# Chunked attention and a Fourier-mixing MLP: the MLP's scheduling priority, the queue of the output DMAs, and the order around the column transform

## The chip, the cores and the metric

The kernel runs on one core of a Trainium2 chip. The metric is the device time of one execution in microseconds (us). The core has TensorE (PE, matmuls and transposes), VectorE (DVE), ScalarE (ACT), GpSimd (POOL) and SyncE (SP, here only a queue that issues DMAs). Each engine works through its own instructions in a fixed order and waits at one whose inputs are not there yet; the engines wait for each other by semaphores. SBUF is the working memory of all engines, PSUM the memory into which TensorE writes; PSUM's buffers are few, and their reuse makes waits.

## The reference

Four batches of 768 rows and 8 heads of 64 (so 512 columns). First an attention in chunks of 32 rows, each chunk looking at 16 rows before it, 8 rows after it and 8 memory rows; then a Fourier mixing, a normalization and an MLP:

```python
for c in range(nc):
    q_c = q[:, :, c_start:c_end]
    k_full = np.concatenate([mem_k, k[:, :, l_start:r_end]], axis=2)
    v_full = np.concatenate([mem_v, v[:, :, l_start:r_end]], axis=2)
    a = softmax(scale * q_c @ k_full.T)
    out[:, :, c_start:c_end] = a @ v_full
x = out.transpose(0, 2, 1, 3).reshape(B, S, H * D)
u = x + np.real(np.fft.fft(np.fft.fft(x, axis=1), axis=2))
un = (u - mean(u)) / np.sqrt(var(u) + 1e-06)
return u + np.maximum(un @ w_ch1, 0.0) @ w_ch2
```

Only float32 goes in and comes out: 4x768x512 is written.

## The kernel before, in words

For each batch there are three stages.

**Attention** (`emit_keys`, `emit_pair`) goes by pairs of heads, four pairs a batch, n = 0 to 15 over all. `emit_keys(n)` loads q, k and v (DMAs on SP's queue), casts q and k to bf16 (L239 into `qb`, L241 into `kb`), copies a shifted part of v (L245, POOL), transposes q on TensorE (L250 into the PSUM tile `trq`), copies it out on ACT (`qT`, L252), transposes k (L256 into `trk`) and copies that out on ACT (`kTb`, L261). `trq` and `trk` have the same tag "tr" with one buffer, so `trk` waits for the copy of `trq`. `emit_pair(n)` then does two halves g: scores (L279, `sc`, one buffer), the exponential (L284, ACT), the product with v (L293, `xa`, one buffer; a float32 matmul is two records in the trace), the reciprocal and the scaled copy on DVE (L297 `zs`, L298 `xsb`), which frees `xa`. In batch 0 the cast of q is DVE's and that of k POOL's; later both are POOL's.

**Fourier mixing** (`emit_fx`): a fold of the batch on DVE for each of two parities (`zy` L313, `pq`, `ff` L321 and L322), split into two float16 parts (`hi` on ACT L326, `lo` on DVE L327), the row transform (`ps`, L335 and L342), its two float16 parts (`up` L349 and L350, `dn` L352), and then for each of six row tiles kt the column transform (`pm`, 8 matmuls, L364), the addition to x on DVE (L368), mean and variance (L370, L371), the subtraction (`un` L373), four transposes (`tp`, L376) and their copy (`unT`, L377). `ps`, `pm` and `tp` share the tag "acc" with two PSUM buffers.

**MLP** (`emit_mlp`): two halves of 384 rows; for each 16 groups of four matmuls (`ph`, L391) with a ReLU on ACT (`hT`, L394), then three groups of 16 matmuls (`pc`, L399), the result on DVE (`osb`, L402) and the output DMA on SP's queue (L404). `ph` and `pc` share the tag "mlp" with two PSUM buffers.

The source emits, for b = 0 to 3, attention(b+1), mixing(b+1) and then MLP(b). A scheduler orders the instructions of each engine: among those that it takes to be ready it picks the one with the highest priority, by default the one that was emitted earlier. So MLP(b), which needs only its own batch, is what fills TensorE while batch b+1 is in attention and mixing. MLP(3) has nothing after it. The weights are loaded by eight DMAs on POOL's queue during attention of batch 0.

Of the kernel before, what the change touches and what calls it, by code (L numbers as in the profile page):

```python
# [10 lines left out]
FP32 = mybir.dt.float32  # L11
BF16 = mybir.dt.bfloat16
FP16 = mybir.dt.float16
# [22 lines left out]
def kernel(  # L36
# [11 lines left out]
    nc = tc.nc  # L48
# [183 lines left out]
    def emit_keys(n):  # L232

        b, pr = seq[n]
        emit_loads(n)
        qb = apool.tile([QP, RB, 2, D], BF16, tag="qb", bufs=1, name="qb")
        kb = apool.tile([KP, RB, 2, D], BF16, tag="kb", bufs=1, name="kb")
        eng = nc.vector if b == 0 else nc.gpsimd
        eng.tensor_copy(qb.rearrange("p j h d -> p h j d"),  # L239
                        qf[n % NS].rearrange("p h (j d) -> p h j d", j=RB))  # L240
        nc.gpsimd.tensor_copy(kb.rearrange("p j h d -> p h j d"),  # L241
                              kf[n % NS].rearrange("p h (j d) -> p h j d", j=RB))
        for hh in range(2):
            v1 = va[(2 * n + hh) % NV]
            nc.gpsimd.tensor_copy(v1[96:128, 0:NT, 0:D + 1], v1[0:32, 1:NB, 0:D + 1])  # L245
        kT = kTb[n % NKT]
        qT = apool.tile([P, S], BF16, tag="qT", bufs=2, name="qT")
        trq = aps.tile([P, S], BF16, tag="tr", bufs=1, name="trq")
        for j in range(RB):
            nc.tensor.transpose(trq[:, j * QP:(j + 1) * QP],  # L250
                                qb[:, j].rearrange("p h d -> p (h d)"), ident_b[0:QP, 0:QP])
        nc.scalar.copy(qT.rearrange("p (a j) -> p a j", j=RB),  # L252
                       trq.rearrange("p (j a) -> p a j", j=RB))
        trk = aps.tile([P, RB * KP], BF16, tag="tr", bufs=1, name="trk")
        for j in range(RB):
            nc.tensor.transpose(trk[:, j * KP:(j + 1) * KP],  # L256
                                kb[:, j].rearrange("p h d -> p (h d)"), ident_b[0:KP, 0:KP])
        nc.vector.tensor_copy(
            kT.rearrange("p (b c) -> p b c", b=NB)[:, 0:NT, 64:72],
            mkT[:, b * (H // 2) + pr, :].unsqueeze(1).to_broadcast([P, NT, NMEM]))  # L260
        nc.scalar.copy(  # L261
            strided(kT, 0, [[BS, NB], [8, 8], [1, RB]]),
            strided(trk, 0, [[8, NB], [1, 8], [KP, RB]]))
        qT_of[n], kT_of[n] = qT, kT

    def emit_pair(n):
        b, pr = seq[n]
        h = 2 * pr
        if b not in xs:
            xs[b] = apool.tile([P, NST, DM], FP32, tag="xsb", bufs=3, name=f"xsb{b}")  # L270
        xb = xs[b]
        qT, kT = qT_of.pop(n), kT_of.pop(n)
        for g in range(2):
            sc = aps.tile([P, 2, 8, 64], FP32, tag="sc", bufs=1, name="sc")
            for t6 in range(6):
                t = 6 * g + t6
                for hh in range(2):
                    r0 = 64 * hh
                    nc.tensor.matmul(sc[:, hh, t6, :], kT[r0:r0 + 64, t * BS:t * BS + P],  # L279
                                     qT[r0:r0 + 64, ts(t, 64)], start=True, stop=True,  # L280
                                     tile_position=(r0, 0))
            e1 = apool.tile([P, 2, 6, 64], FP32, tag="e1", bufs=3, name="e1")
            for half in range(2):
                nc.scalar.activation(e1[:, :, :, ts(half, 32)], sc[:, :, 0:6, ts(half, 32)],  # L284
                                     AFT.Exp, bias=mbias[:, half:half + 1],
                                     scale=1.0 / math.sqrt(D))
            xa = aps.tile([P, 3, 2, 66], FP32, tag="xa", bufs=1, name="xa")
            for st in range(3):
                for hh in range(2):
                    v1 = va[(2 * n + hh) % NV]  # L290
                    for half in range(2):
                        t6 = 2 * st + half
                        nc.tensor.matmul(xa[64 * half:64 * half + 64, st, hh, 0:65],  # L293
                                         e1[:, hh, t6, :], v1[:, 6 * g + t6, 0:65],
                                         start=True, stop=True)
            zs = apool.tile([P, 3, 2], FP32, tag="zs", bufs=3, name="zs")
            nc.vector.reciprocal(zs, xa[:, :, :, 64])  # L297
            nc.vector.tensor_tensor(  # L298
                xb[:, 3 * g:3 * g + 3, h * D:(h + 2) * D].rearrange("p s (h d) -> p s h d", h=2),
                xa[:, :, :, 0:D], zs.unsqueeze(3).to_broadcast([P, 3, 2, D]), ALU.mult)  # L300
# [3 lines left out]
    def emit_fx(b):  # L304
# [48 lines left out]
                rr.append((up.rearrange("p i k s -> p i (k s)"), dn))  # L353
        mu_s = fpool.tile([P, NST, 2], FP32, tag="mu", bufs=2)
        unT = fpool.tile([P, NDT, S], FP16, tag="unT", bufs=2, name="unT")
        for kt in range(NST):
            pm = fps.tile([P, 2, HD], FP32, tag="acc", name="pm")
            for par in range(2):
                im = 0
                for ab in range(2):  # L360
                    rhs = cosD if ab == 0 else (nsinD if kt < 3 else sinD)
                    for part in range(2):
                        lhs = rr[2 * par + ab][kt // 3][:, part, ts(kt % 3, P)]
                        nc.tensor.matmul(pm[:, par, :], lhs, rhs[:, par, :],  # L364
                                         start=(im == 0), stop=(im == 3))
                        im += 1
            uv = xb[:, kt, :].rearrange("p (j c) -> p c j", c=2)
            nc.vector.tensor_tensor(uv, pm, uv, ALU.add)  # L368
            st6 = fpool.tile([P, 6], FP32, tag="st6", bufs=3)
            nc.vector.bn_stats(st6, xb[:, kt, :])  # L370
            nc.vector.bn_aggr(mu_s[:, kt, :], st6)  # L371
            un = fpool.tile([P, DM], FP16, tag="un", bufs=3)
            nc.vector.tensor_scalar(un, xb[:, kt, :], mu_s[:, kt, 0:1], None, ALU.subtract)  # L373
            tp = fps.tile([P, NDT, P], FP16, tag="acc", name="tp")
            for dt in range(NDT):
                nc.tensor.transpose(tp[:, dt, :], un[:, ts(dt, P)], ident_h)  # L376
            nc.vector.tensor_copy(unT[:, :, ts(kt, P)], tp)  # L377
        rstd = fpool.tile([P, NST], FP32, tag="rstd", bufs=2)
        nc.gpsimd.tensor_scalar(rstd, mu_s[:, :, 1], eps, None, ALU.add)  # L379
        nc.gpsimd.tensor_tensor(rstd, rstd, mhalf, ALU.pow)  # L380
# [2 lines left out]
    def emit_mlp(b):  # L383
        xb = xs[b]
        unT, rstd = us[b]
        for sh in range(2):
# [8 lines left out]
            for stl in range(3):  # L395
                st = sh * 3 + stl
                pc = fps.tile([P, DM], FP32, tag="mlp", name="pc")
                for ht in range(NHT):
# [2 lines left out]
                osb = fpool.tile([P, DM], FP32, tag="osb", bufs=3)  # L401
                nc.vector.scalar_tensor_tensor(osb, pc, rstd[:, st:st + 1], xb[:, st, :],  # L402
                                               ALU.mult, ALU.add)
                nc.sync.dma_start(out[b, ts(st, P), :], osb)  # L404

    HP = H // 2

# [13 lines left out]
    for b in range(B):  # L421
        if b + 1 < B:
            emit_attention(b + 1)
            emit_fx(b + 1)
        emit_mlp(b)


# [28 lines left out]
```

## Time and profile before

| | us |
|---|---|
| median of 3 runs (lowest, highest) | 374.26 (372.51, 374.93) |
| the profiled execution | 372.16 |
| its span, from the first to the last instruction | 370.4 |
| TensorE busy | 302.9 (82%) |
| VectorE busy | 196.7 (53%) |
| ScalarE busy | 148.6 (40%) |
| GpSimd busy | 82.6 (22%) |

The profile is of one execution. Its page gives busy time by engine, the span in 40 slices, and the chain of work that ended last: 60% of it is TensorE's, 24% VectorE's. The trace behind it holds each instruction with its start and length and what ended the idle time before it. A matmul's record runs on after the next one has begun, so a stream of matmuls is priced by the length of the whole stream over its count.

### The profile page before, as it was taken

To read this page: it belongs to the slowest core of one execution; us is meant where nothing else is said; L and a number is where in the kernel's file an instruction comes from. 1 tells how busy PE (TensorE), PEld (TensorE's weight loads), DVE (VectorE), ACT (ScalarE), POOL (GpSimd) and SP (SyncE) were. 2 spreads that over 40 slices of the span, in tenths; PEclk is the share of its full clock that TensorE was granted. 3 is DMA by queue.
4 is the path that set the end of the run, shared out by engine and by line. 5 is a ranking of instruction groups with operands and counts; after the bars stand their busy time and mean duration, and the time that the engine had idled before them with its cause. 6 is when DMAs were issued, how large, how long until landed. Compare 5 with 4: busy or idle time off the path is not lost.

```text
span 370.4 us, 6887 instructions
## 1 busy us (share of the span) xinstructions
PE 302.9 (82%) x2848; PEld 188.6 (51%) x2848; DVE 196.7 (53%) x372; ACT 148.6 (40%) x258; POOL 82.6 (22%) x97
## 2 busy tenths in 40 slices
PE   0126661775999999999999999799999994799995
PEld 0125551664755465566554665575545552454542
DVE  8952328966632179787221598763213976541001
ACT  1554441452375166225733642347235430151430
POOL 7712660630064030112730101127000000010000
PEclk9999999987899999999999999999999997699999
DMA  7995699955110230159802004491010000000102
GB/s 132 195 164 114 127 225 196 232 98 127 31 27 2 94 94 2 37 165 180 139 28 80 23 0 126 119 181 22 31 40 18 28 30 28 2 0 28 58 6 79
DMA packets 42022, 30.65 MB, mean 83 GB/s; under 512 B 30216, under 2 KB 32264, under 8 KB 41992
## 3 DMA queue, kind: packets, MB, share of 16 engines
q1 hardware_dynamic: 39304, 26.03, 33.9%
q0 software_dynamic: 2688, 4.19, 6.2%
q8 instruction: 22, 0.36, 0.5%
q14 instruction: 8, 0.07, 0.1%
HBM read 28.11 MB, written 6.29 MB: 93 GB/s over the span
## 4 chain that ended last, share of the span: by engine, by line
PE 60%; DVE 24%; ACT 7%; issue 5%; POOL 2%; SPq 1%; DMA 0%; POOLq 0%; ACTq 0%; DVEq 0%
PE pc L399 17%; PE ph L391 16%; PE xa L293 10%; PE pm L364 6%; DVE zy L313 4%; ACT e L284 3%; PE ps L335 3%; PE sc L279 2%; PE tp L376 2%; DVE pq L315 2%; DVE st L370 2%; DVE lo L327 2%; PE trq L250 2%; DVE xsb L368 2%; DVE pq L316 2%
## 5 line engine op out<-in xcount | busy, mean ns | idle before, releaser
L391 PE MATMUL ph<-unT,w_sb 128*128 128x384 f16 x512 | 95.4, 328 | 1.7 <-DVE osb L402 0.8
L394 ACT ACTIVATE hT<-ph 128x384 f16<-128x384 f32 x128 | 62.1, 492 | 79.8 <-PE ph L391 79.7
L399 PE MATMUL pc<-w_sb,hT 128*128 128x512 f16 x384 | 90.0, 380 | 0.0
L391 PEld LDWEIGHTS <-w_sb 128*128 128x128 f16 x512 | 47.8, 98 | 37.8 <-issue 9.8
L399 PEld LDWEIGHTS <-hT 128*128 128x128 f16 x384 | 35.9, 98 | 38.7 <-issue 0.7
L293 PE MATMUL xa<-va,e 128*64 128x65 f32 x768 | 42.1, 257 | 8.9 <-issue 5.9
L402 DVE SCALAR_TENSOR_TENSOR osb<-pc,rstd,xsb 128x512 f32<-128x512 f32 x24 | 18.0, 748 | 53.2 <-PE pc L399 53.2
L293 PEld LDWEIGHTS xa<-va,e 128*64 128x64 f32 x768 | 33.9, 164 | 21.1 <-issue 16.0
L284 ACT ACTIVATE e<-sc,mbias 128x384 f32<-128x384 f32 x64 | 33.7, 578 | 23.0 <-PE sc L279 22.8
L297 DVE RECIPROCAL zs<-xa 128x6 f32<-128x6 f32 x32 | 6.1, 192 | 61.7 <-PE xa L293 61.6
L245 POOL COPY va<-va 32x780 f32<-32x780 f32 x32 | 28.0, 897 | 39.2 <-DMA va<-in_v_dram 36.5
L252 ACT COPY qT<-trq 128x768 bf16<-128x768 bf16 x16 | 12.8, 798 | 47.1 <-PE trq L250 47.0
L241 POOL CAST kb<-kf 104x1024 bf16<-104x1024 f32 x16 | 19.1, 1196 | 46.0 <-PE ps L335 19.1
L239 POOL CAST qb<-qf 96x1024 bf16<-96x1024 f32 x12 | 13.8, 1149 | 56.0 <-PE trq L250 52.8
L279 PE MATMUL sc<-qT,kTb 64*128 64x64 bf16 x384 | 13.5, 203 | 14.0 <-ACT e L284 7.2
L379 POOL TENSOR_SCALAR rstd<-mu_s 128x6 f32<-128x6 f32 x4 | 1.4, 345 | 104.7 <-DVE mu_s L371 104.7
L368 DVE TENSOR_TENSOR xsb<-pm,xsb 128x512 f32<-128x512 f32 x24 | 16.6, 692 | 11.6 <-PE pm L364 11.6
L349 ACT CAST up<-ps 128x386 f16<-128x386 f32 x16 | 9.6, 601 | 28.0 <-PE ps L335 20.9
L279 PEld LDWEIGHTS <-kTb 64*128 64x128 bf16 x384 | 9.2, 101 | 21.4 <-ACT kTb L261 10.8
L335 PE MATMUL ps<-cosS,hi 128*128 128x193 f16 x48 | 11.0, 276 | 10.9 <-ACT hi L326 10.6
L376 PE MATMUL tp<-ident_h,un 128*128 128x128 f16 x96 | 10.1, 232 | 10.8 <-DVE un L373 10.5
L261 ACT COPY kTb<-trk 128x832 bf16<-128x832 bf16 x16 | 13.6, 851 | 13.1 <-PE trk L256 13.1
(91 smaller groups left out, 378.1 us busy)
## 6 DMA issues: line engine op xcount, KB each, us to landing
qf<-in_q_dram SPq DMA_DIRECT2D x16, 384.0 KB, 5.2
kf<-in_k_dram SPq DMA_DIRECT2D x16, 384.0 KB, 6.2
out_dram<-osb SPq DMA_DIRECT2D x24, 256.0 KB, 2.0
va<-in_v_dram SPq DMA_DIRECT2D x32, 144.0 KB, 5.9
w_sb<-in_moe_w_ch_dram POOLq DMA_DIRECT2D x8, 512.0 KB, 14.8
va<-in_v_dram SPq DMA_DIRECT2D x32, 48.0 KB, 5.7
va<-in_mem_v_dram SPq DMA_DIRECT2D x32, 24.0 KB
mkf<-in_mem_k_dram SPq DMA_DIRECT2D x1, 64.0 KB
```

The lines of the kernel that those rows point to most:

```text
L241: nc.gpsimd.tensor_copy(kb.rearrange("p j h d -> p h j d"), kf[n % NS].rearrange("p h (j d) -> p h j d", j=RB))
L245: nc.gpsimd.tensor_copy(v1[96:128, 0:NT, 0:D + 1], v1[0:32, 1:NB, 0:D + 1])
L279: nc.tensor.matmul(sc[:, hh, t6, :], kT[r0:r0 + 64, t * BS:t * BS + P], qT[r0:r0 + 64, ts(t, 64)], start=True, stop=True, tile_position=(r ...
L284: nc.scalar.activation(e1[:, :, :, ts(half, 32)], sc[:, :, 0:6, ts(half, 32)], AFT.Exp, bias=mbias[:, half:half + 1], scale=1.0 / math.sqr ...
L293: nc.tensor.matmul(xa[64 * half:64 * half + 64, st, hh, 0:65], e1[:, hh, t6, :], v1[:, 6 * g + t6, 0:65], start=True, stop=True)
L335: nc.tensor.matmul(ps[:, sp, :], part[:, ab, sp * 3 + st, :], tab[:, sp, st, :], start=(st == 0 and i == 0), stop=(st == 2 and i == 1))
L364: nc.tensor.matmul(pm[:, par, :], lhs, rhs[:, par, :], start=(im == 0), stop=(im == 3))
L368: nc.vector.tensor_tensor(uv, pm, uv, ALU.add)
L391: nc.tensor.matmul(ph[:, 0:384], w1_sb[:, dt, ts(ht, P)], unT[:, dt, sh * 384:(sh + 1) * 384], start=(dt == 0), stop=(dt == NDT - 1))
L394: nc.scalar.activation(hT[:, ht, :], ph[:, 0:384], AFT.Relu)
L399: nc.tensor.matmul(pc, hT[:, ht, ts(stl, P)], w2_sb[:, ht, :], start=(ht == 0), stop=(ht == NHT - 1))
L402: nc.vector.scalar_tensor_tensor(osb, pc, rstd[:, st:st + 1], xb[:, st, :], ALU.mult, ALU.add)
```

## The change

Four things. In batch 0 the cast of k is DVE's too, `trk` lies in the "acc" buffers and `xa` of the second half in the "mlp" buffers. The eight matmuls of `pm` for row tile kt+1 are emitted ahead of the addition for tile kt. The output DMAs are issued by ACT's queue. `emit_mlp` is emitted with a priority below all the rest.

```diff
-        nc.gpsimd.tensor_copy(kb.rearrange("p j h d -> p h j d"),
-                              kf[n % NS].rearrange("p h (j d) -> p h j d", j=RB))
+        eng.tensor_copy(kb.rearrange("p j h d -> p h j d"),
+                        kf[n % NS].rearrange("p h (j d) -> p h j d", j=RB))
...
-        trk = aps.tile([P, RB * KP], BF16, tag="tr", bufs=1, name="trk")
+        if b == 0:
+            trk = fps.tile([P, RB * KP], BF16, tag="acc", name="trk")
+        else:
+            trk = aps.tile([P, RB * KP], BF16, tag="tr", bufs=1, name="trk")
...
-            xa = aps.tile([P, 3, 2, 66], FP32, tag="xa", bufs=1, name="xa")
+            if b == 0 and g == 1:
+                xa = fps.tile([P, 3, 2, 66], FP32, tag="mlp", name="xa")
+            else:
+                xa = aps.tile([P, 3, 2, 66], FP32, tag="xa", bufs=1, name="xa")
...
-        for kt in range(NST):
+        def columns(kt):
             pm = fps.tile([P, 2, HD], FP32, tag="acc", name="pm")
...
+            return pm
+
+        pm = columns(0)
+        for kt in range(NST):
+            nxt = columns(kt + 1) if kt + 1 < NST else None
             uv = xb[:, kt, :].rearrange("p (j c) -> p c j", c=2)
             nc.vector.tensor_tensor(uv, pm, uv, ALU.add)
...
             nc.vector.tensor_copy(unT[:, :, ts(kt, P)], tp)
+            pm = nxt
...
-                nc.sync.dma_start(out[b, ts(st, P), :], osb)
+                nc.scalar.dma_start(out[b, ts(st, P), :], osb)
...
-        emit_mlp(b)
+        with tc.high_priority(offset=-100000):
+            emit_mlp(b)
```

What it does to the order on the engines shows at three places. The first is VectorE around a pair of heads in batch 0, before and then now (`qf0_76`, `kf0_79` are the loaded q and k of the last pair, `xa_507` and `xa_539` the two halves of the pair before it).

```order
L297 RECIPROCAL zs_520<-xa_507 128x6
L239 CAST qb_463<-qf0_76 96x2x8x64
L298 TENSOR_TENSOR xsb0_280<-xa_507,zs_520 128x3x128
L297 RECIPROCAL zs_552<-xa_539 128x6
L298 TENSOR_TENSOR xsb0_280<-xa_539,zs_552 128x3x128
```

```order
L303 RECIPROCAL zs_520<-xa_507 128x6
L239 CAST qb_463<-qf0_76 96x2x8x64
L304 TENSOR_TENSOR xsb0_280<-xa_507,zs_520 128x3x128
L241 CAST kb_464<-kf0_79 104x2x8x64
L303 RECIPROCAL zs_552<-xa_539 128x6
L304 TENSOR_TENSOR xsb0_280<-xa_539,zs_552 128x3x128
```

The cast of k stands on VectorE between the two halves. On TensorE the transposes of q, which stood between the twelve products `xa` of the first half and the twelve of the second, now stand behind nine of the second half's.

The second place is VectorE at the first row tiles of the last batch's column transform, before and then now (`xsb3_2852` is that batch; a new number in `pm_`, `un_` or `tp_` is a new row tile's).

```order
L368 TENSOR_TENSOR xsb3_2852<-pm_3293,xsb3_2852 128x2x256
L370 BN_STATS st6_3303<-xsb3_2852 128x6
L371 BN_AGGR mu_s_3291<-st6_3303 128x2
L373 TENSOR_SCALAR un_3306<-xsb3_2852,mu_s_3291 128x512
L377 COPY unT_3292<-tp_3308 128x4x128
L368 TENSOR_TENSOR xsb3_2852<-pm_3314,xsb3_2852 128x2x256
L370 BN_STATS st6_3324<-xsb3_2852 128x6
```

```order
L379 TENSOR_TENSOR xsb3_2852<-pm_3293,xsb3_2852 128x2x256
L381 BN_STATS st6_3312<-xsb3_2852 128x6
L379 TENSOR_TENSOR xsb3_2852<-pm_3302,xsb3_2852 128x2x256
L382 BN_AGGR mu_s_3291<-st6_3312 128x2
L381 BN_STATS st6_3333<-xsb3_2852 128x6
L384 TENSOR_SCALAR un_3315<-xsb3_2852,mu_s_3291 128x512
L382 BN_AGGR mu_s_3291<-st6_3333 128x2
L384 TENSOR_SCALAR un_3336<-xsb3_2852,mu_s_3291 128x512
L388 COPY unT_3292<-tp_3317 128x4x128
L379 TENSOR_TENSOR xsb3_2852<-pm_3323,xsb3_2852 128x2x256
L388 COPY unT_3292<-tp_3338 128x4x128
L381 BN_STATS st6_3354<-xsb3_2852 128x6
```

The addition of the second tile now comes ahead of the first tile's copy of its transposes, and so on through the six. On TensorE, between the first `pm` and the last `tp` of that batch, 39 matmuls `ph` of MLP(3) stood before, all of them behind the third tile; now 28 matmuls `pc` of MLP(2) and 12 `ph` of MLP(3) stand there, spread over all the tiles.

The third place is ScalarE in the mixing of batch 2, now (before, no DMA stood on it).

```order
L332 CAST hi<-ff 128x1536
L416 DMA out_dram<-osb 128x512
L252 COPY qT<-trq 128x768
L355 CAST up<-ps 128x2x193 x2
L264 COPY kTb_89<-trk 128x13x64
```

The 24 output DMAs stand between ScalarE's other work, each with its wait for `osb`; SyncE's queue holds the loads alone.

## Rows read from the trace of the kernel before

**Rows 1.** The page: part 1 (TensorE) and part 2 (granted clock in 40 slices), one group of part 5.
```profile
PE 302.9 (82%) x2848; PEld 188.6 (51%) x2848; DVE 196.7 (53%) x372; ACT 148.6 (40%) x258; POOL 82.6 (22%) x97
...
PEclk9999999987899999999999999999999997699999
...
L402 DVE SCALAR_TENSOR_TENSOR osb<-pc,rstd,xsb 128x512 f32<-128x512 f32 x24 | 18.0, 748 | 53.2 <-PE pc L399 53.2
```

**Rows 2.** Busy time by stage: window, its length, then each engine's busy us, clock, DMA share.
```profile
81.30:106.10 24.80, 19.64 (x250) 13.88 (x249) 16.74 (x42) 10.29 (x20) 3.05 (x4) 0.86 0.34 69
106.10:304.60 198.50, 191.69 (x1803) 113.84 (x1801) 108.92 (x187) 90.37 (x161) 39.04 (x42) 1.00 0.31 67
```

**Rows 3.** Timeline of TensorE, batch 0: start, length, instruction, [idle before it <-releaser].
```profile
28.13 1.31 PE L293 MATMUL xa<-va,e 128*64 128x65 f32 x18 [0.98 <-DVE xsb L298]
...
43.61 1.57 PE L293 MATMUL xa<-va,e 128*64 128x65 f32 x24
46.04 0.82 PE L250 MATMUL trq<-ident_b,qb 96*128 96x96 bf16 x8 [0.86 <-DVE qb L239]
...
48.30 0.88 PE L256 MATMUL trk<-ident_b,kb 104*128 104x104 bf16 x8
```

**Rows 4.** Timeline of all engines, batch 0: casts of q on VectorE.
```profile
9.92 2.24 DVE L239 CAST qb<-qf 96x1024 bf16<-96x1024 f32 x1
...
36.69 0.65 DVE L239 CAST qb<-qf 96x1024 bf16<-96x1024 f32 x1
```

**Rows 5.** Timeline of VectorE, mixing of batch 0.
```profile
71.23 0.58 DVE L350 TENSOR_TENSOR up<-ps,up 128x386 f16<-128x386 f32 x1
...
81.35 0.69 DVE L368 TENSOR_TENSOR xsb<-pm,xsb 128x512 f32<-128x512 f32 x1
...
105.67 0.42 DVE L377 COPY unT<-tp 128x512 f16<-128x512 f16 x1 [0.49 <-PE tp L376]
```

**Rows 6.** Groups by line, VectorE, 57 to 107 us: busy us, mean ns, idle before.
```profile
L368 DVE TENSOR_TENSOR xsb<-pm,xsb 128x512 f32<-128x512 f32 x6 | 4.2, 692 | 3.5 <-PE pm L364 3.5
L370 DVE BATCH_NORM_STATS2 st<-xsb 128x6 f32<-128x512 f32 x6 | 4.1, 688 | 0.1
...
L373 DVE TENSOR_SCALAR un<-xsb,mu_s 128x512 f16<-128x512 f32 x6 | 2.9, 482 | 0.1
...
L298 DVE TENSOR_TENSOR xsb<-xa,zs 128x384 f32<-128x384 f32 x5 | 2.7, 546 | 0.0
...
L377 DVE COPY unT<-tp 128x512 f16<-128x512 f16 x6 | 2.5, 425 | 3.5 <-PE tp L376 3.5
...
L371 DVE BATCH_NORM_AGGREGATE mu_s<-st 128x2 f32<-128x6 f32 x6 | 1.1, 176 | 0.1
```

**Rows 7.** Timeline of TensorE, mixing of batch 3 and the end.
```profile
306.11 0.27 PE L364 MATMUL pm<-nsinD,up 128*128 128x256 f16 x1
309.19 0.40 PE L376 MATMUL tp<-ident_h,un 128*128 128x128 f16 x4 [2.81 <-DVE un L373]
...
312.71 0.61 PE L376 MATMUL tp<-ident_h,un 128*128 128x128 f16 x4 [2.25 <-DVE un L373]
...
329.40 0.40 PE L376 MATMUL tp<-ident_h,un 128*128 128x128 f16 x4
...
345.34 10.53 PE L391 MATMUL ph<-unT,w_sb 128*128 128x384 f16 x60 [0.19 <-DVE osb L402]
355.71 10.52 PE L399 MATMUL pc<-w_sb,hT 128*128 128x512 f16 x48
```

**Rows 8.** Timeline of TensorE, attention of batch 2.
```profile
165.79 0.92 PE L293 MATMUL xa<-va,e 128*64 128x65 f32 x24
```

**Rows 9.** Waits of SyncE's queue: who waited for whom, us in total, times, longest.
```profile
SPq L404 <- DVE osb L402: 191.5, 21, 31.0
```

**Rows 10.** Waits of all engines, same columns.
```profile
DVE osb L402 <- PE pc L399: 53.2, 15, 14.1
```

**Rows 11.** The output DMA's line: issue time in ns, min/median/max.
```profile
L404 SPq DMA_DIRECT2D out_dram<-osb x24: 332/333/375, 119.8 to 367.0; - x24
```

More of the change, by code (lines that the diff above doesn't have):

```diff
@@ L366, in emit_fx @@
                         im += 1
+            return pm
+        pm = columns(0)
+        for kt in range(NST):
+            nxt = columns(kt + 1) if kt + 1 < NST else None
             uv = xb[:, kt, :].rearrange("p (j c) -> p c j", c=2)
             nc.vector.tensor_tensor(uv, pm, uv, ALU.add)
-            st6 = fpool.tile([P, 6], FP32, tag="st6", bufs=3)
+            st6 = fpool.tile([P, 6], FP32, tag="st6", bufs=3, name="st6")
             nc.vector.bn_stats(st6, xb[:, kt, :])
             nc.vector.bn_aggr(mu_s[:, kt, :], st6)
-            un = fpool.tile([P, DM], FP16, tag="un", bufs=3)
+            un = fpool.tile([P, DM], FP16, tag="un", bufs=3, name="un")
             nc.vector.tensor_scalar(un, xb[:, kt, :], mu_s[:, kt, 0:1], None, ALU.subtract)
```

## The prediction

> **What bounds the kernel now.** I read the page first: TensorE is busy for 302.9 of the span's 370.4 us, so 67.5 us of the span are without a matmul [rows 1]. Busy time by stage then says where. From 106.1 to 304.6 us TensorE is busy for 191.69 of 198.5 us [rows 2]: in this stretch the MLP of one batch fills what attention and mixing of the next leave free, and only 6.8 us are idle. So the 60 us outside it are what a change of order can win, and there are three such places: attention of batch 0, which has no MLP beside it; the column transform of batch 0, the same; and the mixing of batch 3, which should have MLP(2) beside it but has used it up.
>
> In **attention of batch 0** the timeline of TensorE shows a loop of waits, not of work. The products `xa` of a second half wait 0.98 us for VectorE's copy of the first half, because `xa` has one buffer; `trq` waits 0.86 us for the cast of q [rows 3]. The granted clock of this stretch prints as 9 [rows 1], but the rows speak for the lower of the two levels (1.2 GHz): 24 records of `xa` take 1.57 us here [rows 3] and 0.92 us in batch 2 [rows 8].
>
> In the **column transform of batch 0** each row tile is a chain: `pm`, addition, statistics, `un`, `tp`, `unT`, and only then the next `pm`. From the first addition at 81.35 to the end of the last copy, 105.67 + 0.42, are 24.7 us [rows 5], 4.1 a tile, of which VectorE idles 3.5 us for `pm` and 3.5 for `tp` [rows 6], with TensorE idle 5.2 us and its mean clock at 0.86 [rows 2]. In batch 3 the same chain stands bare: after the last `pm` matmul (306.11 + 0.27) TensorE idles 2.81 us to the first `tp`, 2.25 to the next [rows 7] and 2.25 again a tile later, each ended by VectorE's `un`; the page's clock falls to 7 and 6 tenths there [rows 1]. The last `tp` group begins at 329.40.
>
> **The change, part by part.**
>
> *Batch 0's attention.* The first `xa` group begins at 43.61 and ends at 45.18; the second, freed of the copy, follows at once. Nine of its twelve products take 0.75 x 1.57 = 1.18, `trq` 0.82, the other three 0.39: `trk` can begin at 47.6. It needs the cast of k, now third on VectorE after the reciprocal: q's cast 0.65 [rows 4], the copy 0.55 [rows 6], k's 0.65 end at about 47.2, in time. `trk` began at 48.30 [rows 3], so 0.7 to 0.8 us are won in each of two pairs. The first pair wins 0.9 in the same way (0.98 of wait gone, the casts in its place), the last the whole 0.95 at its end, with no casts behind it. Sum: **-3.4**. From GpSimd, which casts k now, nothing is won: it was not waited for. The bound below is the waits themselves, 4 x 0.98 = -3.9. Above it is the cast when GpSimd works on SBUF beside it: the cast of q that took 0.65 took 2.24 at 9.92 us [rows 4]. With 1.6 more in three pairs the term is +1.4. I take 0.65, because GpSimd has fewer casts to do now and its copies of v do not fall at a fixed place. The Trainium skill (SBUF — State Buffer, "SBUF: two separate sides") says that VectorE and GpSimd share a port pair as an exclusive lock, the loser blocked for the whole instruction: by that rule the upper end would be the common case, and the whole sum 4.8 us smaller; the two lengths in rows 4 agree with it, and no row of this case shows how often it would hit.
>
> *Mixing of batch 0 up to `pm`.* The second parity's last fold now comes ahead of a piece of `up` (0.58 [rows 5]), so `hi`, `lo` and `ps` come some 0.5 earlier: **-0.5**, between 0 and -0.6.
>
> *Column transform of batch 0.* With `pm` a tile ahead, VectorE no longer waits for it, and its other work stands where it waited for `tp`. What is left is its own work: 0.692 + 0.688 + 0.176 + 0.482 + 0.425 = 2.46 us a tile [rows 6], 14.8 for six, with attention's three copies (3 x 0.55 [rows 6]) 16.4; 1.3 more I put for the short instructions beside them and the first tile. 24.7 becomes 17.7: -7.0. But TensorE gets less done meanwhile. Counted in the two orders up to the last `tp`, it has issued 13 `ph`, 24 `sc`, 14 `xa` and 10 transposes fewer, and must do them later, where it is the bound: 13 x 10.53/60 = 2.3 [rows 7], 14 x 2 records x 0.92/24 = 1.1 [rows 8], the small rest about 1.3 by the same spacing: 4.7. Net **-2.3**. Bounds: -6 (the extra work falls into the 6.8 us of idle time), and +4.7 (the loop not shorter at all).
>
> *Mixing of batch 3.* From 306.4 to 329.4 are 23.0 us, in which TensorE did 39 `ph`, 39 x 0.176 = 6.9. In the changed order 28 `pc` (10.52/48 = 0.219 each [rows 7]) and 12 `ph` stand there, 8.2 us, and the loop goes at VectorE's pace: 14.8, two `osb` at 0.75 [rows 1], and 0.7 put for waits on `pc`: 17.0. Time not spent on MLP: 16.1 before, 8.8 after: **-7.3**. This is also where the clock comes back, and it is counted in it. Bounds: -10.6 (all the idle time and slow matmuls gone), -1 (the loop keeps its 4 us).
>
> *Mixing of batches 1 and 2:* their loops were filled with MLP already [rows 2]; they are as much VectorE's as TensorE's now. **0**, between -6.8, all idle time of that stretch, and +4.
>
> *Output DMAs on ScalarE.* On SyncE they wait 191.5 us for `osb`, in 21 waits [rows 9], with the loads of q, k and v behind them; GpSimd and VectorE take the loads late, but TensorE has MLP to do, so freeing them is worth 0. On ScalarE each issue takes 0.33 us [rows 11], 24 of them 8.0; behind them stand `qT`, `kTb`, `e`, `up` and `hT`. ScalarE is 40% busy and its order was laid with them, so I put **+1** on the path, of the bounds 0 and 8.
>
> *Lowest priority of the MLP* has no instruction of its own; its effect is in the counts above. Sum: -3.4 - 0.5 - 2.3 - 7.3 + 1 = **-12.5**. The profiled execution took 372.16 us, which gives 359.7. It lies 2.1 under the median of the runs and just below the lowest, 372.51; the forecast is **360 us**.
>
> **The rivals.**
>
> *Two buffers are not enough.* `pm`, the next `pm` and `tp` share two "acc" buffers, so a tile ahead could wait for the buffer and the chain stay at 4 us. For it: the same gap came in every tile [rows 7]. Against it: in the order, the next addition comes before the copy of `tp`, and it is the addition that frees a buffer. Then the terms are -3.4 - 0.5 + 4.7 - 1 + 1 = +0.8: 373 us, no change. The Trainium skill (Perfetto Trace Analysis, "Optimization Strategy") says that consistent bubbles can mean too little PSUM for the next tile: rows 7 show such bubbles, ended by `un`, not by a buffer. Chance 0.08.
>
> *ScalarE stands at its DMAs: slower.* VectorE waited 53.2 us in 15 waits for `pc` ahead of `osb`, 3.5 us on average, up to 14.1 [rows 10]. If ScalarE comes to a DMA that early, it stands 3.5 + 0.75 + 0.33 = 4.6, 24 times 110 us, and everything of attention behind it with it. It decides from 13.5/24 = 0.56 us a DMA that reach TensorE; with 1 us each, 24 in place of 1, the time is 383. Against it: each DMA stands in the order about where its `osb` ends. Chance 0.07.
>
> *Idle time goes in the middle too.* With loads not queued behind outputs and mixing a tile ahead, the 6.8 us between 106 and 304 [rows 2] go as well: 353. For it: the blocked queue [rows 9]. Against it: with MLP work at hand, late loads did not stop TensorE. Chance 0.15.
>
> **How the numbers follow.** The forecast has 0.70, with a range of its own of 354 to 366. 350 to 368 takes in the third rival and the forecast's bounds (half of the two column terms missing gives 364.5, the cast's upper end the same), and leaves out the other two and some tails. I call 1% (3.7 us) what a measurement of this kernel can tell from no change. Faster: 0.70 x 0.97 + 0.15, **0.83**; slower: **0.07**; within: **0.10**, the buffers' rival and the forecast's upper tail.
>
> **What would show it.** The row tiles of batch 0 at about 2.9 us from addition to addition in place of 4.1, and TensorE's idle time in batch 3's mixing down from 7 us to under 3, with no fall of the clock; batch 0's mixing begun 3.4 us earlier; the last stretch, from the last `tp` to the end, longer than before by some 5 us (27 more `ph`), since that much of MLP(3) is left. Wrong would be: waits on ScalarE ahead of `qT`, `e` or `up` ended by VectorE's `osb`; `pm` ended by `xsb` or `unT`; casts of k of over 1 us in batch 0.

## The result and the profile after

The changed kernel takes **362.67 us** (median of 4 runs, 362.4 to 363.51), the kernel before 373.81 (4 runs of the same job, 372.51 to 374.93): a ratio of 0.971 (95% interval 0.967 to 0.974). The forecast was 360, its range 350 to 368. The profiled span went from 370.4 to 360.8 us. Cut at the same marks in both, its 9.6 us come from here:

| piece of the span | before | after | difference |
|---|---|---|---|
| start to the first fold (`zy`) of batch 0 | 57.23 | 56.14 | -1.1 |
| to batch 0's first addition | 24.12 | 25.09 | +1.0 |
| column transform of batch 0, to the end of the last `unT` | 24.74 | 15.52 | -9.2 |
| the middle, to the last `pm` matmul ahead of batch 3's first `tp` | 200.3 | 204.65 | +4.4 |
| column transform of batch 3, to the last `tp` | 23.0 | 13.72 | -9.3 |
| to the end | 41.0 | 45.68 | +4.7 |

The page: part 1 (TensorE) and the clock of part 2, and what answers to rows 2, by windows (length, each engine's busy us, clock, DMA share, GB/s): batch 0's column transform, the middle, batch 3's column transform.
```profile
PE 300.4 (83%) x2848; PEld 186.3 (52%) x2848; DVE 196.1 (54%) x376; ACT 148.6 (41%) x258; POOL 81.4 (23%) x93
...
PEclk9999985589999999999999998999999999999998
```
```profile
81.20:96.80 15.60, 13.75 (x198) 10.32 (x198) 14.64 (x39) 6.24 (x12) 2.18 (x3) 1.00 0.15 30
96.80:301.40 204.60, 194.71 (x1865) 116.34 (x1860) 113.09 (x195) 95.44 (x171) 43.98 (x44) 0.99 0.30 70
301.40:315.60 14.20, 13.55 (x99) 8.08 (x97) 13.09 (x31) 1.26 (x3) 0.84 (x2) 1.00 0.06 21
```
Both transforms now have TensorE and VectorE busy for 88 to 95% of their time, at a granted clock of 1.00. In batch 3 the gaps of 2.81 and 2.25 us ahead of `tp` [rows 7] are gone; `pc` stands in them. TensorE's timeline there (start, length, instruction, idle before it and what ended that):
```profile
301.25 2.54 PE L411 MATMUL pc<-w_sb,hT 128*128 128x512 f16 x11
303.80 0.40 PE L387 MATMUL tp<-ident_h,un 128*128 128x128 f16 x4
...
306.72 1.89 PE L411 MATMUL pc<-w_sb,hT 128*128 128x512 f16 x8
...
315.12 0.39 PE L387 MATMUL tp<-ident_h,un 128*128 128x128 f16 x4
```
From the first `tp` to the last are 11.32 us for five tiles, 2.26 a tile; the forecast had 2.46, the sum of VectorE's records. In VectorE's timeline a record starts a little before the last one ends (306.64 against 306.04 + 0.68), so the sum overstates it:
```profile
306.04 0.68 DVE L381 BATCH_NORM_STATS2 st<-xsb 128x6 f32<-128x512 f32 x1
306.64 0.73 DVE L414 SCALAR_TENSOR_TENSOR osb<-pc,rstd,xsb 128x512 f32<-128x512 f32 x1
```
In attention of batch 0 the waits of rows 3 did not go; they changed their owner. TensorE's timeline:
```profile
33.78 0.48 PE L299 MATMUL xa<-va,e 128*64 128x65 f32 x4
35.05 2.43 PE L299 MATMUL xa<-va,e 128*64 128x65 f32 x38 [0.79 <-ACT e L287]
37.48 0.82 PE L250 MATMUL trq<-ident_b,qb 96*128 96x96 bf16 x8
...
38.87 0.87 PE L259 MATMUL trk<-ident_b,kb 104*128 104x104 bf16 x8
...
40.68 0.50 PE L282 MATMUL sc<-qT,kTb 64*128 64x64 bf16 x12 [0.94 <-ACT kTb L264]
...
49.51 0.35 PE L282 MATMUL sc<-qT,kTb 64*128 64x64 bf16 x12 [0.94 <-ACT kTb L264]
```
Only two products (four records) run, then TensorE stands 0.79 us for the exponential of the second half; a pair takes 8.8 to 9.0 us (31.70, 40.68, 49.51), where it took 8.6 before. The order shows why (TensorE, first pair; `e_294` is the exponential of the first half, `e_326` of the second):
```
L299 MATMUL xa<-va_82,e_294 64x65 x2
...
L299 MATMUL xa<-va_82,e_326 64x65 x2
L299 MATMUL xa<-va_83,e_294 64x65 x2
L299 MATMUL xa<-va_82,e_294 64x65 x2
```
A product of the second half stands among those of the first. In the kernel before, where `xa` has one buffer, all twelve of the first half stand ahead of the second's; with its own buffer the scheduler was free to put one between them, and TensorE, which goes in order, stands at it.

In the middle TensorE's idle time grew from 6.8 us [rows 2] to 9.9. The new waits stand ahead of the row transform `ps`, for `hi`, and before `hi` are VectorE's fold pieces, beside which GpSimd now works. TensorE, then VectorE, then GpSimd, batch 2's mixing:
```profile
216.10 0.34 PE L341 MATMUL ps<-cosS,hi 128*128 128x193 f16 x1 [2.42 <-ACT hi L332]
```
```profile
206.67 2.22 DVE L319 TENSOR_TENSOR zy<-xsb 128x1536 f32<-128x1536 f32 x1
208.92 1.67 DVE L321 TENSOR_TENSOR pq<-zy 128x768 f32<-128x768 f32 x1
210.52 1.58 DVE L322 TENSOR_TENSOR pq<-zy 128x768 f32<-128x768 f32 x1
```
```profile
208.18 1.60 POOL L241 CAST kb<-kf 104x1024 bf16<-104x1024 f32 x1 [0.91 <-DMA kf<-in_k_dram]
209.85 2.95 POOL L245 COPY va<-va 32x780 f32<-32x780 f32 x2
```
In the kernel before the same three took 1.76, 0.96 and 0.95 us (at 209.25 to 212.86), with GpSimd idle from 209.23. The loads are no longer behind the outputs on SyncE, so GpSimd's share comes earlier, and meets the folds.

The output DMAs on ScalarE, by their line (ns, min/median/max; issue times) and the only wait put down to them (us, times, longest; against rows 9):
```profile
L416 ACTq DMA_DIRECT2D out_dram<-osb x24: 338/338/378, 114.9 to 357.4; - x24
```
```profile
ACT qT L252 <- DMA out_dram<-osb: 1.6, 1, 1.6
```

### The profile page after: what moved, and what is told of

It reads as the page before. It is cut to its first block, busy times and chain, and to the rows that moved or that the text cites. A ratio compares the mean times of both kernels' runs of the same rounds, so it can differ in the third digit from the quotient of the medians.

```text
span 360.8 us, 6878 instructions
## 1 busy us (share of the span) xinstructions
PE 300.4 (83%) x2848; PEld 186.3 (52%) x2848; DVE 196.1 (54%) x376; ACT 148.6 (41%) x258; POOL 81.4 (23%) x93
## 4 chain that ended last, share of the span: by engine, by line
PE 71%; DVE 13%; ACT 8%; issue 3%; POOL 2%; DMA 2%; SPq 1%; ACTq 0%; POOLq 0%; DVEq 0%
PE pc L411 23%; PE ph L403 20%; PE xa L299 9%; PE ps L341 5%; PE pm L370 5%; ACT e L287 3%; PE sc L282 2%; DVE zy L319 2%; ACT hi L332 2%; PE tp L387 2%; PE trq L250 2%; PE trk L259 2%; DMA va<-in_v_dram 2%; DVE pq L322 1%; DVE pq L321 1%
## 5 line engine op out<-in xcount | busy, mean ns | idle before, releaser
L411 PE MATMUL pc<-w_sb,hT 128*128 128x512 f16 x384 | 93.1, 380 | 0.0
L411 PEld LDWEIGHTS <-hT 128*128 128x128 f16 x384 | 35.1, 98 | 35.5 <-issue 0.5
L245 POOL COPY va<-va 32x780 f32<-32x780 f32 x32 | 31.0, 986 | 44.8 <-DMA va<-in_v_dram 41.1
L332 ACT CAST hi<-ff 128x1536 f16<-128x1536 f32 x8 | 11.8, 1472 | 19.1 <-DVE ff L328 16.0
L341 PEld LDWEIGHTS <-hi 128*128 128x128 f16 x96 | 9.7, 107 | 18.3 <-ACT hi L332 17.9
L304 DVE TENSOR_TENSOR xsb<-xa,zs 128x384 f32<-128x384 f32 x32 | 17.7, 554 | 0.8
L355 ACT CAST up<-ps 128x386 f16<-128x386 f32 x16 | 9.6, 599 | 18.0 <-PE ps L341 13.7
## 6 DMA issues: line engine op xcount, KB each, us to landing
w_sb<-in_moe_w_ch_dram POOLq DMA_DIRECT2D x8, 512.0 KB, 13.7
```

Of the source, the lines that this page charges most:

```text
L304: nc.vector.tensor_tensor(xb[:, 3 * g:3 * g + 3, h * D:(h + 2) * D].rearrange("p s (h d) -> p s h d", h=2), xa[:, :, :, 0:D], zs.unsqueeze ...
L332: nc.scalar.copy(hi.rearrange(fl), ff.rearrange(fl))
L341: nc.tensor.matmul(ps[:, sp, :], part[:, ab, sp * 3 + st, :], tab[:, sp, st, :], start=(st == 0 and i == 0), stop=(st == 2 and i == 1))
L411: nc.tensor.matmul(pc, hT[:, ht, ts(stl, P)], w2_sb[:, ht, :], start=(ht == 0), stop=(ht == NHT - 1))
```

## The experiments

Eleven kernels were run, all beside the kernel before (median 372.6 to 373.3 in their jobs). "Pinned" is the changed kernel with the edit of the first one.

**1. The second half's products behind all of the first's.** The buffers stay; only the order in batch 0 is fixed.
```diff
+            with tc.issue_after(last_xa.ins) if b == 0 and g == 1 else ExitStack():
                 for st in range(3):
...
-                            nc.tensor.matmul(xa[64 * half:64 * half + 64, st, hh, 0:65],
+                            last_xa = nc.tensor.matmul(xa[64 * half:64 * half + 64, st, hh, 0:65],
```


> The changed kernel with one thing added: in batch 0 the products xa of a second half are issued behind all twelve of the first half. Theory (the second PSUM buffer let two products of the second half slip ahead of ten of the first, and TensorE stands 0.8 to 0.9 us for their exponential in each pair): the wait in front of the 38-record xa group goes, a pair of heads takes about 8.0 in place of 9.0 us, and the time is 358.5 to 360 against 362.7 of the changed kernel. Rival (the pairs are bound by the chain kTb, sc, e and not by this wait): 362 to 363, the wait only moves in front of sc.

Measured: **357.23 us** (356.64 to 358.75), ratio 0.961 (0.954 to 0.967): 5.4 us under the changed kernel, 4.3 when each is taken against the kernel before in its own job, and faster than was expected. TensorE's timeline of the same pair:
```profile
32.42 0.51 PE L282 MATMUL sc<-qT,kTb 64*128 64x64 bf16 x12 [1.15 <-ACT e L287]
32.86 2.43 PE L300 MATMUL xa<-va,e 128*64 128x65 f32 x38
...
36.35 0.54 PE L259 MATMUL trk<-ident_b,kb 104*128 104x104 bf16 x8
...
37.84 0.35 PE L282 MATMUL sc<-qT,kTb 64*128 64x64 bf16 x12 [0.95 <-ACT kTb L264]
```
The wait is gone and pairs take 7.0 us (30.77, 37.84, 44.81). So it was the order, not the buffers, that kept the gain away. The wait is 0.8 of the 2.0 us a pair; for most of the rest the rows speak for TensorE's higher clock level: `trk` takes 0.54 us in place of 0.87 above. Why the clock rose earlier here is not shown, and neither the forecast nor the expectation had it: from the start to the first `zy` the pinned kernel takes 50.3 us, 6.9 under the kernel before, where the forecast had 3.4.

**2. Outputs back on SyncE**, all else as changed.
```diff
-                nc.scalar.dma_start(out[b, ts(st, P), :], osb)
+                nc.sync.dma_start(out[b, ts(st, P), :], osb)
```


> The changed kernel with its output DMAs issued by SyncE again. Theory (loads that are no longer queued behind outputs arrive while VectorE folds batches 1 and 2, and GpSimd's casts and copies of v then slow the folds by about 2.4 us each, with TensorE idle behind them): the folds of batch 2 go back to 0.96 us a piece, the 2.42 us in front of ps go, and the time is 359 to 362, not slower than 362.7. Rival (outputs on ScalarE were a gain, since the loads were late behind them): 364 to 368. Second rival (ScalarE's standing at the DMAs cost the lost microseconds): 358 to 360, with waits of hT and e shorter.

Measured: **400.24 us**, ratio 1.076 (1.067 to 1.084): a miss for all that was expected, by far. Waits of SyncE's queue (us, times, longest), and TensorE by window (columns as above):
```profile
SPq L416 <- DVE osb L414: 163.0, 20, 39.1
SPq L123 <- PE xa L299: 107.3, 12, 18.1
```
```profile
160.00:235.00 75.00, 46.27 (x547) 35.95 (x544) 50.05 (x97) 23.35 (x36) 24.37 (x23) 0.70 0.26 61
```
The loads of v wait for `xa`, outputs stand behind them, and the MLP that fills TensorE stops: in the order it stands at `ph` 128 and `pc` 80 from the last `tp` of batch 1's column transform to the last `tp` of batch 2's. TensorE is busy 46.27 of 75 us there, at a clock of 0.70. With this priority, in this kernel, the outputs need a queue of their own.

**3. The MLP's ordinary priority**, outputs on ScalarE.
```diff
-        with tc.high_priority(offset=-100000):
-            emit_mlp(b)
+        emit_mlp(b)
```


> The changed kernel with the MLP at its default priority. Theory (the low priority keeps MLP(2) back as work beside the mixing of batch 3): the column transform of batch 3 stands bare again but with pm a tile ahead, about 17 us with 6 to 8 of them idle on TensorE, the time 368 to 372. Rival (the lead of pm alone gives the gain): 362 to 364.

Measured: **361.9 us** (360.43 to 361.96), ratio 0.973 (0.966 to 0.980), the same as with it, as the rival had it. At the first `pm` of batch 3 the order has issued 255 `pc` in place of 260. The theory falls: the priority is worth nothing here.

**4. Without the lead**: `pm` emitted in its own tile again.
```diff
-        pm = columns(0)
         for kt in range(NST):
-            nxt = columns(kt + 1) if kt + 1 < NST else None
+            pm = columns(kt)
```


> The changed kernel with the column matmuls of a row tile emitted in its own turn again. Theory (the lead takes pm out of the chain of a tile and is worth about 9 us in batch 0 less 4.7 us of matmuls not done meanwhile, and something in batch 3): the column transform of batch 0 takes 22 to 25 us again in place of 15.5, the time is 367 to 371. Rival (with the MLP at the lowest priority the chains are filled anyway, except batch 0's): 363 to 367.

Measured: **370.5 us**, ratio 0.994 (0.990 to 0.997): the lead is worth 8 us. In batch 3 a tile takes 3.5 us though 48 `pc` stand in the loop (TensorE's timeline):
```profile
307.36 0.40 PE L386 MATMUL tp<-ident_h,un 128*128 128x128 f16 x4
...
310.88 0.40 PE L386 MATMUL tp<-ident_h,un 128*128 128x128 f16 x4
```

**5. The lead alone**, on the kernel before.
```diff
-        for kt in range(NST):
+        def columns(kt):
...
+        pm = columns(0)
+        for kt in range(NST):
+            nxt = columns(kt + 1) if kt + 1 < NST else None
...
+            pm = nxt
```


> The kernel before with one part of the change alone: pm emitted a row tile ahead (outputs on SyncE, default priority, batch 0 as before). Theory (the lead is nearly all of the gain: without it the changed kernel took 370.5): 363 to 366, the column transform of batch 0 in 15 to 17 us, that of batch 3 in 14 to 17 us with some idle time left. Rival (the lead pays only with MLP work kept back for batch 3's mixing): 368 to 371.

Measured: **364.42 us** (363.9 to 365.0), ratio 0.978 (0.974 to 0.981): 9 of the whole change's 11 us. Its order has issued all 288 `pc` by batch 3's first `pm`, so that mixing stands bare: TensorE's idle time ahead of the first `tp` is 2.35 us, and it is busy 11.91 of 16.4 us there.

**6. Without the three edits of batch 0.**
```diff
-        eng.tensor_copy(kb.rearrange("p j h d -> p h j d"),
+        nc.gpsimd.tensor_copy(kb.rearrange("p j h d -> p h j d"),
...
-        if b == 0:
+        if False:
             trk = fps.tile([P, RB * KP], BF16, tag="acc", name="trk")
...
-            if b == 0 and g == 1:
+            if False:
                 xa = fps.tile([P, 3, 2, 66], FP32, tag="mlp", name="xa")
```


> The changed kernel with the three edits in batch 0's attention undone (k's cast, trk's and xa's buffers). Theory (as made they are worth about 1 us: mixing of batch 0 begins at 56.14 in place of 57.23, since the wait for the second half's exponential takes what the buffers give): 363 to 365. Rival (as made they are a loss, a pair of heads being 0.4 us longer): 360.5 to 362. Second rival (they are worth the 3.4 us that were forecast): 365.5 to 367.

Measured: **362.14 us** (361.65 to 363.23), the same as the changed kernel. As made, these edits bring nothing: in the traces they start the first `zy` 1.25 us earlier (56.14, here 57.39), and the stretch from there to the first addition takes 2.4 us more (25.1, here 22.7).

**7. v's shifted copy on ScalarE** in batches 1 to 3, pinned, to take GpSimd from beside the folds.
```diff
+            if b == 0:
                 nc.gpsimd.tensor_copy(v1[96:128, 0:NT, 0:D + 1], v1[0:32, 1:NB, 0:D + 1])
+            else:
+                nc.scalar.copy(v1[96:128, 0:NT, 0:D + 1], v1[0:32, 1:NB, 0:D + 1])
```


> The pinned kernel (357.2) with the shifted copy of v done by ScalarE in batches 1 to 3 in place of GpSimd. Theory (GpSimd's copies beside VectorE's folds stretch those in the mixing of batches 1 and 2, and TensorE's waits for hi of 1.5 and 2.7 us there follow from it): the fold's pieces of 768 columns take 0.96 us wherever no cast of q or k runs beside them, the two waits shrink to under 1 us together, 352.5 to 355.5. Rival (the casts of q and k on GpSimd do the same, or 24 more copies on ScalarE delay hT and e): 357 to 361.

Measured: **368.85 us**, ratio 0.988 (0.982 to 0.993), 11.6 slower than pinned, a miss. ScalarE's timeline, then TensorE's:
```profile
132.60 0.84 ACT L248 COPY va<-va 32x780 f32<-32x780 f32 x1
133.46 0.58 ACT L290 ACTIVATE e<-sc,mbias 128x384 f32<-128x384 f32 x1
133.94 0.48 ACT L410 ACTIVATE hT<-ph 128x384 f16<-128x384 f32 x1
```
```profile
134.47 0.65 PE L407 MATMUL ph<-unT,w_sb 128*128 128x384 f16 x3 [1.66 <-ACT hT L410]
```
The copy stands between exponentials, `hT` comes late and TensorE pauses: from 97 to 300 us its waits for `hT` are 5.4 us, 1.4 pinned. Its granted clock is 0.933 on the mean in the profiled run, the slowest of the four, and 0.947 to 0.956 in the others (pinned 0.957 to 0.964). The order changed as well: 57, 144 and 240 `pc` are out by the first `pm` of batches 1, 2 and 3, where the pinned kernel has 76, 157 and 260, and no run parts the two.

**8. Pinned, outputs on SyncE, ordinary priority**: the edits of 2 and 3 on top of 1.
```diff
-                nc.scalar.dma_start(out[b, ts(st, P), :], osb)
+                nc.sync.dma_start(out[b, ts(st, P), :], osb)
...
-        with tc.high_priority(offset=-100000):
-            emit_mlp(b)
+        emit_mlp(b)
```


> The pinned kernel with the outputs on SyncE and the MLP at default priority again. Theory (the outputs on SyncE do harm only together with the low priority, where they keep osb's buffers full; alone, late loads are covered by the MLP): 356 to 359. Rival (moving the outputs to ScalarE is a gain of its own): 361 to 366. With e1 it prices the two parts together.

Measured: **364.57 us**, ratio 0.978 (0.975 to 0.982): 7.3 above pinned, as the rival had it. Batch 0's last `tp` ends at 90.4 us as in pinned (90.9); by the last `tp` of batch 3 it is 10 us behind (319.5 against 309.4). As in 5, all 288 `pc` have been issued by batch 3's first `pm`; TensorE's timeline there:
```profile
307.53 0.40 PE L388 MATMUL tp<-ident_h,un 128*128 128x128 f16 x4 [2.14 <-DVE un L385]
...
313.01 0.40 PE L388 MATMUL tp<-ident_h,un 128*128 128x128 f16 x4 [1.18 <-DVE un L385]
```
Its counts in that mixing are those of 5 (no `pc`, 22 `ph`), but the granted clock is 0.84 there and was 1.00 in 5, and the stretch from the first `pm` to the last `tp` takes 17.1 us in place of 15.2.

**9. Pinned with ordinary priority**, outputs on ScalarE: the edit of 3 on top of 1.
```diff
-        with tc.high_priority(offset=-100000):
-            emit_mlp(b)
+        emit_mlp(b)
```


> The pinned kernel without the low priority: the changed kernel with the second group's xa matmuls of batch 0 held behind the first group's, outputs still issued by ScalarE, the MLP at its ordinary priority. It parts the 7.3 us that the pinned kernel lost when outputs went back to SyncE and the priority was taken away at once. Theory: the issuing engine alone is worth it, since TensorE's order keeps 33 pc matmuls of the third MLP for the last mixing without the priority too (28 with it, none with outputs on SyncE): 355.5 to 359.5 us. Rival: the priority is worth something once batch 0 is in order, because it holds more of the MLP back in every batch: 360 to 364 us.

Measured: **356.58 us** (354.85 to 357.69), ratio 0.956 (0.951 to 0.960), as pinned. With 8 this prices the issuing engine alone, order and all: 364.57 - 356.58 = 8.0 us. It leaves 33 `pc` for batch 3's mixing, where TensorE is busy for 16.23 of 16.9 us.

**10. v's shifted rows loaded a second time**, pinned, with no copy in batches 1 to 3.
```diff
+            if b == 0:
                 nc.gpsimd.tensor_copy(v1[96:128, 0:NT, 0:D + 1], v1[0:32, 1:NB, 0:D + 1])
...
+            if b > 0:
+                nc.sync.dma_start(v1[96:128, 0:NT - 1, 0:D], ...)
+                nc.sync.dma_start(v1[96:112, NT - 1, 0:D], ...)
```


> The pinned kernel with v's shifted copy in batches 1 to 3 loaded a second time by SyncE from memory, so that GpSimd copies v only in batch 0 (24 copies of 0.8 to 1.5 us fewer, 48 loads more). It tries the cause that I give for what the middle lost: VectorE's fold pieces run beside GpSimd's copies (zy 2.33 and pq 1.67 and 1.59 us beside them, 1.76 and 0.96 us without, one pair in the trace of the pinned kernel), so the cast hi is late and TensorE stands before ps. Theory: with the copies gone the pieces take their short time and the wait before ps falls from 2.7 us a batch to about 0.7, some 4 us over the batches with the clock's fall: 351 to 355.5 us. Rival: hi waits on the attention's last normalisation, not on the folds, or the loads (smaller packets, more issues on SyncE) come late: 356 to 360 us. If the loads hold up the attention, over 361 us.

Measured: **405.92 us** (404.54 to 411.76), ratio 1.089 (1.083 to 1.094): a miss. GpSimd's timeline, then TensorE's:
```profile
109.09 1.04 POOL L247 CAST qb<-qf 96x1024 bf16<-96x1024 f32 x1 [18.92 <-DMA qf<-in_q_dram]
```
```profile
146.16 0.34 PE L351 MATMUL ps<-cosS,hi 128*128 128x193 f16 x1 [4.55 <-ACT hi L342]
```
Loads come late, and the order changed as well: all of an MLP has been issued before the next batch's first `pm` (`pc` 96, 192, 288), so the mixings stand bare. The two cannot be parted here, and the run says nothing about the folds.

**11. v's shifted copy cut to 2 of 65 columns** in batches 1 to 3, pinned; the order's counts stay. This leaves work out.
```diff
-            nc.gpsimd.tensor_copy(v1[96:128, 0:NT, 0:D + 1], v1[0:32, 1:NB, 0:D + 1])
+            c = D + 1 if b == 0 else 2
+            nc.gpsimd.tensor_copy(v1[96:128, 0:NT, 0:c], v1[0:32, 1:NB, 0:c])
```


> The pinned kernel in which GpSimd's shifted copy of v takes 2 of the 65 columns in batches 1 to 3 (63 columns of the shifted rows stay from batch 0: the work is left out). TensorE's order keeps the same counts as the pinned kernel at every mixing (pc 76, 157 and 260 at the first pm of batches 1, 2 and 3), which the version with a second load did not (96, 192, 288), so this tries the collision of VectorE's folds with GpSimd's copies by itself. Theory: with next to nothing of the copies left, the zy and pq pieces before the last ps of each attention take 1.76 and 0.96 us, TensorE waits 1 to 2 us less before ps in each of three batches and its clock stays up: 351.5 to 355 us, at least 2 us under the pinned kernel's 357.2. Rival: the casts of q and k come to stand beside the folds in the copies' place, and hi is as late as before: 355.5 to 358.5 us.

Measured: **352.57 us** (351.9 to 354.11), ratio 0.946 (0.941 to 0.952), 4.7 under pinned. The size is as expected, the place is not: 3.5 of the 3.7 us between the two profiled spans stand in batch 0's mixing, before the first `pm`. VectorE there, where GpSimd works for batch 1's first pairs (pinned, a copy of v from 56.91 to 58.88 and a cast of q from 60.34; here the cast begins at 60.77, behind both pieces shown), pinned and then this one:
```profile
58.11 2.39 DVE L334 TENSOR_TENSOR lo<-ff,hi 128x1536 f16<-128x1536 f32 x1
60.53 1.67 DVE L322 TENSOR_TENSOR pq<-zy 128x768 f32<-128x768 f32 x1
```
```profile
57.47 1.76 DVE L335 TENSOR_TENSOR lo<-ff,hi 128x1536 f16<-128x1536 f32 x1
59.26 0.96 DVE L323 TENSOR_TENSOR pq<-zy 128x768 f32<-128x768 f32 x1
```
and by window from the first `ps` to the first `pm` of batch 0, pinned, this one, and experiment 9:
```profile
58.00:74.60 16.60, 12.57 (x112) 10.44 (x113) 12.53 (x13) 6.88 (x10) 6.27 (x6) 0.65 1.07 196
```
```profile
57.30:70.90 13.60, 10.20 (x112) 8.79 (x113) 11.16 (x13) 6.86 (x10) 4.46 (x6) 0.80 1.21 193
```
```profile
58.60:72.60 14.00, 9.91 (x112) 8.54 (x113) 11.87 (x13) 6.91 (x10) 7.27 (x6) 0.81 1.16 184
```
The collision is real, but the 3 us here are mostly not its price. Experiment 9 has the full copies, up to here the same order as pinned, and the same long `lo` and `pq` (2.39 and 1.67 us); it takes 14.0 us, 0.4 more than this one. What it shares with this one is the clock (0.81 and 0.80, pinned 0.65), which differed between two executions of the same instructions. From there to the first `pm` of batch 3 both take 218.6 us: the wait ahead of batch 2's `ps` fell from 2.74 to 1.85, but the clock dipped to 0.88 in that mixing (205.8 to 220.2). So less of the 4.7 us than it seems is the copies', and how much is open.

## Why the prediction was right or wrong

The sum was -12.5 on the span, and the span fell by 9.6. The sign and the main cause held; several terms were off, in both directions. That the sum came within 2.9 us is in part luck: three pieces fell short by 2.3, 1.5 and 5.6, and the two column transforms (2.2 and 3.3) and the output DMAs (1) made up for 6.5 of it.

**Attention of batch 0, forecast -3.4, measured -1.1: the step that failed.** "The second, freed of the copy, follows at once" took for granted that the order keeps the first half's products together. It does not, and a buffer more put a wait for the second exponential inside. Experiment 1 shows it: pinned, the mixing's `ps` begins at 58.0 in place of 64.0, though part of these 6 us is TensorE's clock, as said there. The forecast counted in the order that nine of twelve products came ahead of `trq`, not which half's came first. The casts of k on VectorE, the upper bound of this term, took what the forecast chose (0.65), all four of them (their line, ns, min/median/max):
```profile
L241 DVE CAST kb<-kf x4: 677/682/711, 14.2 to 46.9; 104x1024 bf16<-104x1024 f32 x4
```
The rule weighed against that choice, the Trainium skill's lock between VectorE and GpSimd (SBUF — State Buffer, "SBUF: two separate sides"), was not put to the test there: beside three of these casts GpSimd had neither a cast nor a copy under way, and beside the fourth (46.86) it began one at 47.42, 0.12 us before the end. The folds of 1.67 in place of 0.96 us above agree with it.

**Mixing of batch 0 up to `pm`, forecast -0.5, measured +1.0.** The earlier fold did not bring `ps` forward: a `pq` took 1.59 us in place of 0.95, beside a copy of v that GpSimd had begun at 58.34, and from the first `zy` to `ps` are 7.8 us in place of 7.2. VectorE's timeline, before and after:
```profile
59.97 0.95 DVE L316 TENSOR_TENSOR pq<-zy 128x768 f32<-128x768 f32 x1
```
```profile
58.88 1.59 DVE L322 TENSOR_TENSOR pq<-zy 128x768 f32<-128x768 f32 x1
```
The rest is TensorE's clock. The granted clock that is printed for this stretch (0.93 before, 0.61 after) misleads, as it did in attention: in the trace of the kernel before it is printed as full up to 71.8 us, where the rows speak for the lower level. By the length of the records (about 0.37 us at the lower level, 1.2 GHz, and 0.25 at the higher), 42 of the 60 `ps` ran at the lower level before and 52 after. In experiment 5, whose instructions are up to here those of the kernel before in the same order, 20 did, and the stretch took 22.7 us in place of 24.1. So the clock moves this piece by more than the +1.0 from one execution to the next, and the sign of the term is not shown. TensorE's timeline before, after, and in 5:
```profile
77.16 0.37 PE L335 MATMUL ps<-cosS,lo 128*128 128x193 f16 x1
```
```profile
76.48 0.37 PE L341 MATMUL ps<-cosS,lo 128*128 128x193 f16 x1
```
```profile
76.58 0.25 PE L341 MATMUL ps<-cosS,lo 128*128 128x193 f16 x1
```

**Column transform of batch 0, forecast 17.7 long, measured 15.5**: mechanism right, the gain 2.2 larger. **Batch 3's, forecast 17.0, measured 13.7**: right, at the lower bound of -10.6 for the term. Both were sized at 2.46 us a tile plus allowances; a tile takes 2.26 to 2.6, since records overlap. Experiments 4 and 5 show that the lead makes them, 8 to 9 us of the change.

**Output DMAs on ScalarE, forecast +1: wrong in sign.** ScalarE stood at them once, for 1.6 us. What they won is in the order for the most part: with SyncE 287 or 288 `pc` are out by batch 3's first `pm` (before, 5, 8), with ScalarE 240 to 260 (4, 9, 3, after), and those left over fill that mixing. It is no rule (10 has ScalarE and 288 out, 2 has SyncE and 144). On the unpinned kernel with batch 0's old code this is worth 2.3 us (6 against 5; priority included, which 3 and 9 price at nothing), on the pinned one 8.0. The profiled spans of 8 and 9 are 10.3 us apart: 33 `pc` more and 8 `ph` fewer are left for batch 3's mixing, 5.8 us at the prices of rows 7, and 2.7 us stand in batch 0's mixing, where both have the same order and 9 had the higher clock. So 8.0 is likely too high a price for the queue, and that the freed loads won nothing is not shown. That the scheduler holds more of the MLP back when ScalarE issues is read from the orders; why it does was not tried.

**Lowest priority: "its effect is in the counts above" was wrong.** The counts are there without it (3, 9). Its one shown effect is on SyncE, where it costs 36 us (2 against 5, which differ by batch 0's edits as well, worth nothing by 6).

**The middle, forecast 0, lost 5.6.** By the forecast's own prices the middle had 4.7 more to do and 27 `pc` less (5.9), so -1.2; it took +4.4. 0.9 of the loss is where the cut lies, since 16 `pm` now stand ahead of batch 3's first `tp` in place of 8. 3.1 is idle time of TensorE, ahead of `ps` for `hi` above all, and this wait came with the outputs' queue: in the mixings of batches 1 and 2 it is 1.2 and 3.0 us in 9, none and 0.3 in 8. That the folds are slower beside GpSimd is shown; that this is what the middle lost is not. Experiment 11 took the copies away and won nothing between batch 0's and batch 3's `pm`. And in 5, the lead alone, no fold piece of batches 1 to 3 is lengthened (`pq` at most 0.96), yet the middle takes 209.8 us with all 288 `pc` in it, 9.5 more than before, where 4.7 of work had been priced as moved there. So the lead brings a like loss without the collision. What it is stays open.

**The end**: 27 more `ph`, +4.7 as forecast.

Of the rivals, two "acc" buffers were enough (15.5 us for six tiles), ScalarE did not stand at its DMAs, and the middle's idle time grew in place of going. Of the signs named, the shorter tiles of batch 0 (2.6 us), batch 3 without gaps and without a fall of the clock, and the longer end came; batch 0's mixing 3.4 us earlier did not.

The best kernels here are the pinned ones, 356.6 and 357.2 us: by the ratios to the kernel before, 1.0 to 1.5% under the change as made, for one constraint of order.

## What to carry to other kernels

A buffer that lifts a wait also lifts an order. Look in the new order at which instruction comes first behind the old wait: on an engine that goes in order, one that comes too early brings back the whole wait under another name. And filler work is worth most in the last stage that has nothing else: count how much of it is left when that stage begins, since edits that look unrelated (which engine issues a DMA) move that count.

## What the runs showed of the hardware

VectorE's pieces took up to 2.8 times as long beside GpSimd's casts and copies: `pq` 1.67 in place of 0.96 us in the changed kernel (2.66 in experiments 3, 4 and 7), `zy` 2.22 in place of 1.76, `lo` 2.39 in place of 1.76 (experiment 1). Which of the two began first went with it: in the changed kernel's trace eight pieces are lengthened, and each began while GpSimd was at a cast or copy; the five others that ran beside one for over 0.1 us had begun before it and kept their time.

A DMA issue on ScalarE took 338 ns, on SyncE 332 [rows 11].

In batch 0 the level of TensorE's clock differed between executions of the same instructions in the same order: from the first `zy` to the first addition the kernel before took 24.1 us and experiment 5 22.7, experiment 8 25.6 and experiment 9 22.9. A difference of 1 to 2 us in that stretch says little of a change.
